# First norm of a transformer block on Trainium2: VectorE sums tiles 0, 1 and 3 and ScalarE tile 2, and two weight loads change places

## The chip, the cores and the metric

One core of a Trainium2 chip. The experiments ran on three chips (e1 to e4, e5 to e8, and e9 to e12), each group with the kernel before beside it. The metric is the device time of one execution in microseconds (us). A run in the "fast" state is one without a visible slowdown of the chip. Executions of one kernel differ by about 0.1% (the kernel before: 830.95 to 832.09 us), and the trace of single executions ("looks": one profiled execution of each kernel) has to show the mechanism.

## The reference

```python
x   = A_x                                   # 2048 rows of 1024, bf16
mod = silu(c) @ w_mod                       # six vectors: sa, ca, ga, sb, cb, gb
h   = layernorm(x) * (1 + ca) + sa          # "the first norm"
qkv = h @ wqkv
...                                         # linear attention, 32 heads, with elu+1 features
x   = x + ga * attention(...)
h   = layernorm(x) * (1 + cb) + sb
x   = x + gb * ((silu(h @ w_gate) * (h @ w_up)) @ w_down)
```

## The kernel before

The rows are worked in four chunks of four tiles of 128 rows. Only the head of the program is changed: the first norm of chunk 0, and the loads in front of the q products. For each tile a statistic, a term `(var + eps) ** -0.5` (a power on GpSimd), and a normalisation are made; TensorE transposes the tile; the scale `1 + ca` is multiplied in when the transposed tile is copied out of PSUM. The scale itself is made by TensorE in one-column products (`mod_sc`), from the weights `WCA` in two halves of 512 columns. `warm` issues dummy matmuls. A k-tile is 128 of the 1024 columns over which a product sums, so q's products need the scaled tile and the weights of all eight k-tiles.

```python
ca_load(0)                 # scale weights, columns 0-511
wq_load(0, 2)              # q weights, k-tiles 0, 1
ca_load(1)                 # scale weights, columns 512-1023
wq_load(2, 2)
wq_load(4, 2)
sa_load(1)                 # shift weights
...
warm(13, bank=3)
act_stats(1)               # ScalarE: sum and sum of squares of tile 1
for f in s0_: f()          # VectorE: statistics of tile 0
ln1_rstd1(0)               # its term
s2_[0](); s2_[1]()         # VectorE: statistics of tile 2
act_xn(0, MV[:, 0, 0:1])   # ScalarE normalises tile 0; VectorE makes its bias first
tile_transposes(0)
warm(5, bank=3)
act_var(1)
s2_[2]()
...                        # terms of tiles 1 and 2
s3_[0](); s3_[1](); s3_[2]()
ln1_rstd1(3)
act_xn(1, SUMX[:, 1:2])
ln1_xn(2)                  # VectorE normalises tile 2
tile_transposes(2)
mod_sc(WCA, 8, range(2))   # first scale columns (0-255)
ln1_xn(3)
fin_ca(0, 2)
tile_transposes(1, 3)
mod_sc(WCA, 8, range(2, 4))  # second scale columns (256-511)
h0_first(0, "dve")
...
# q products of chunk 0
for nts, dts in ((range(4), (0,)), (range(4), (1,)), ((4, 5, 6), (0, 1))):
    for nt in nts: q_part(nt, qb[nt], dts)
mod_sc(WCA, 8, range(4, 8))  # columns 512-1023
fin_ca(4, 4)
for dt in (4, 5): h0_scale_only(dt)
for nt in range(7): q_part(nt, qb[nt], (2, 3))
```

VectorE runs its instructions in the order written here.

## Time and profile before

| | before |
|---|---|
| time, median of 3 | 831.19 us (831.15 to 832.09) |
| span of the profiled execution | 829.4 us |
| TensorE busy | 824.0 us |
| first transpose of tile 0 | 8.76 us |
| first q product | 12.43 us |

The head of the profile page of the kernel before, busy time of each engine with its share of the span:

```profile
PE 824.0 (99%) x4083; PEld 378.4 (46%) x4083; DVE 312.0 (38%) x665; ACT 197.6 (24%) x336; POOL 39.8 (5%) x57
```

TensorE is busy practically always. So the question for any change here is not how much work VectorE loses, but when TensorE's unbroken work begins and what is in it.

TensorE's timeline of the kernel before: start, length, what it ran and how often, and in brackets the idle time before it with what ended that.

```profile
2.61 5.72 PE L176 MATMUL ps<-e,ident 128*128 128x512 bf16 x13 [0.24 <-DVE e L176]
8.76 0.62 PE L176 MATMUL ps<-ident,xres 128*128 128x128 bf16 x8 [0.42 <-ACT xres L176]
9.21 1.24 PE L176 MATMUL ps<-e,ident 128*128 128x512 bf16 x5
10.29 0.61 PE L176 MATMUL ps<-ident,xres 128*128 128x128 bf16 x8
10.74 0.54 PE L176 MATMUL ps<-siluc,wca 128*128 128x1 bf16 x16
11.14 1.05 PE L176 MATMUL ps<-ident,xres 128*128 128x128 bf16 x16
12.03 0.54 PE L176 MATMUL ps<-siluc,wca 128*128 128x1 bf16 x16
12.43 3.18 PE L176 MATMUL ps<-ht,wqk 128*128 128x512 bf16 x14
15.45 0.94 PE L176 MATMUL ps<-siluc,wca 128*128 128x1 bf16 x32
16.25 4.91 PE L176 MATMUL ps<-ht,wqk 128*128 128x512 bf16 x22
```

Lines `ps<-e,ident` are dummies, `ps<-ident,xres` transposes, `ps<-siluc,wca` scale columns, and `ps<-ht,wqk` q products. From 8.76 us on each line starts where the one before it has issued its last, with no idle time: five dummies fill 9.21 to 10.29 us, and 22 matmuls of 512 columns fill 16.25 to 21.00, 216 ns each.

The chain of waits of the kernel before, from its start in order of time (start, length, what). `xres` is a tile of rows, `stats` its statistics, `mv` their aggregate (mean and variance), `ve` the variance plus eps, and `nmr` the bias of ScalarE's normalisation:

```profile
1.71 4.21 DMA xres<-in_A_x_dram
...
5.94 1.29 DVE stats L176 x2
7.22 0.11 DVE nmr L176
7.34 0.14 DVE mv L176
7.47 1.23 ACT xres L176
...
8.76 818.08 PE ps L176 x4069
```

The chain reads: tile 2 lands at 5.92 us, VectorE takes its statistics, only then makes the bias of tile **0** (`nmr`), ScalarE normalises tile 0, and TensorE starts.

The DMA view of the kernel before, for the one issue at 2.65 us (KB, and us from issue to landing):

```profile
wca<-in_w_mod_dram SPq DMA_DIRECT2D x1, 1024.0 KB, 7.8
```

The first half of the scale weights landed at about 2.65 + 7.8 = 10.45 us, 0.3 us before its use at 10.74.

### The profile page before, as it was taken

How to read it: one execution, taken by the hardware profiler on the slowest of the kernel's cores; microseconds unless marked ns; L12 is line 12 of the kernel's file. 1: busy time of each engine (PE TensorE's matmuls, PEld its weight loads, DVE VectorE, ACT ScalarE, POOL GpSimd, SP SyncE). 2: the span in 40 equal slices, each digit the busy share in tenths (PEclk: the TensorE clock that was granted, in tenths of full speed). 3: DMA queues.
4: the chain of work that ended last, by engine and by line, in shares of the span. 5: the costliest groups of instructions: out<-in, count | busy, mean ns of one | idle time of the engine just before them, and what ended most of it. 6: DMA issues, size and time to landing. Idle time of an engine off the chain costs nothing.

```text
span 829.4 us, 10017 instructions
## 1 busy us (share of the span) xinstructions
PE 824.0 (99%) x4083; PEld 378.4 (46%) x4083; DVE 312.0 (38%) x665; ACT 197.6 (24%) x336; POOL 39.8 (5%) x57
## 2 busy tenths in 40 slices
PE   8999999999999999999999999999999999999998
PEld 4544444454444444444444444444444444444444
DVE  5797986756955521121221111122111111221111
ACT  4757641323242111011111101111110111111011
POOL 1010000000130000030000003000000300000000
PEclk9999999999999999999999999999999999999999
DMA  9969655928397996700455570045557004553000
GB/s 320 288 151 229 149 159 172 202 102 304 60 258 225 259 267 174 192 25 14 128 150 155 150 188 28 15 126 153 153 153 187 26 18 125 154 151 86 0 26 26
DMA packets 199245, 119.28 MB, mean 144 GB/s; under 512 B 57880, under 2 KB 182944, under 8 KB 199200
## 3 DMA queue, kind: packets, MB, share of 16 engines
q1 hardware_dynamic: 199184, 118.65, 52.7%
q8 instruction: 32, 0.52, 0.3%
q14 instruction: 13, 0.11, 0.0%
q10 hardware_dynamic: 16, 0.00, 0.0%
HBM read 100.67 MB, written 4.33 MB: 127 GB/s over the span
## 4 chain that ended last, share of the span: by engine, by line
PE 99%; DMA 1%; DVE 0%; ACT 0%; SPq 0%; issue 0%
PE ps L176 99%; DMA xres<-in_A_x_dram 1%; DVE stats L176 0%; ACT xres L176 0%; SPq L176 0%; DVE xres L176 0%; DVE mv L176 0%; DVE nmr L176 0%
## 5 line engine op out<-in xcount | busy, mean ns | idle before, releaser
L176 PE MATMUL ps<-h2t,gug 128*128 128x512 bf16 x896 | 211.7, 379 | 0.0
L176 PE MATMUL ps<-h2t,guu 128*128 128x512 bf16 x896 | 211.7, 379 | 0.0
L176 DVE TENSOR_TENSOR at<-sg,ps 128x512 bf16<-128x512 bf16 x112 | 77.1, 688 | 282.7 <-PE ps L176 281.1
L176 ACT ACTIVATE sg<-ps 128x512 bf16<-128x512 f32 x112 | 66.9, 597 | 309.7 <-PE ps L176 309.7
L176 PEld LDWEIGHTS ps<-h2t,guu 128*128 128x128 bf16 x896 | 87.5, 98 | 105.8
L176 PEld LDWEIGHTS ps<-h2t,gug 128*128 128x128 bf16 x896 | 87.4, 98 | 105.7
L176 PE MATMUL ps<-wd_a,at 128*128 128x512 bf16 (+1 forms) x512 | 112.4, 378 | 0.0
L176 PE MATMUL ps<-ht,wqk 128*128 128x512 bf16 x512 | 111.7, 379 | 0.0
L176 PE MATMUL ps<-wd_b,at 128*128 128x512 bf16 (+1 forms) x384 | 85.0, 378 | 0.0
L176 PEld LDWEIGHTS ps<-wd_a,at 128*128 128x128 bf16 x512 | 50.0, 98 | 59.8
L176 DVE TENSOR_TENSOR ut<-att,gb_b 128x512 bf16<-128x512 bf16 (+1 forms) x32 | 13.8, 430 | 167.5 <-ACT att L176 167.5
L176 PEld LDWEIGHTS ps<-ht,wqk 128*128 128x128 bf16 x512 | 49.4, 98 | 58.8
L176 ACT ACTIVATE att<-ps 128x512 bf16<-128x512 f32 (+1 forms) x32 | 17.4, 591 | 182.1 <-PE ps L176 182.1
L176 PEld LDWEIGHTS ps<-wd_b,at 128*128 128x128 bf16 x384 | 37.5, 98 | 44.7
L176 PE MATMUL ps<-pk,xres 128*128 128x512 bf16 x256 | 56.5, 379 | 0.0
L176 PE MATMUL ps<-mw,pqt 128*128 128x512 bf16 x256 | 56.3, 379 | 0.0
L176 POOL TENSOR_SCALAR h2t<-h2t,modcol 128x512 bf16<-128x512 bf16 x32 | 26.4, 841 | 383.0 <-DMA h2t<-xn 383.0
L176 ACT ACTIVATE e<-ps 128x512 bf16<-128x512 f32 x56 | 33.1, 603 | 31.7 <-PE ps L176 20.5
L176 PEld LDWEIGHTS ps<-mw,pqt 128*128 128x128 bf16 x256 | 24.8, 98 | 30.3 <-DVE xres L176 0.4
L176 PEld LDWEIGHTS ps<-pk,xres 128*128 128x128 bf16 x256 | 24.8, 98 | 30.0 <-issue 0.4
L176 ACT ACTIVATE junk<-xres 128x1024 bf16<-128x1024 bf16 x24 | 25.4, 1058 | 35.1 <-DVE xres L176 34.9
L176 DVE SCALAR_TENSOR_TENSOR xres<-ps,xres 128x512 bf16<-128x512 f32 x32 | 21.4, 689 | 12.3 <-PE ps L176 11.7
(107 smaller groups left out, 346.0 us busy)
## 6 DMA issues: line engine op xcount, KB each, us to landing
gug<-in_B_w_gate_dram SPq DMA_DIRECT2D x56, 512.0 KB, 3.9
guu<-in_B_w_up_dram SPq DMA_DIRECT2D x56, 512.0 KB, 5.2
xres<-in_A_x_dram SPq DMA_DIRECT2D x20, 256.0 KB, 7.8
rb<-recip_den SPq DMA_DIRECT2D x8, 512.0 KB, 11.5
stgx<-in_w_mod_dram SPq DMA_DIRECT2D x2, 2048.0 KB, 7.8
wd_a<-in_B_w_down_dram SPq DMA_DIRECT2D x4, 1024.0 KB, 7.8
out_dram<-xres SPq DMA_DIRECT2D x31, 128.0 KB, 1.7
xres<-in_A_x_dram SPq DMA_DIRECT2D x3, 1024.0 KB, 14.0
```

Source lines behind the costliest of these rows:

```text
L176: return getattr(e, method)(**kw)
```

## The change

The intent: VectorE takes tiles 0 and 1 as soon as they land, back to back, and makes both terms in one step; ScalarE takes tile 2; two dummies fewer; the q weights of k-tiles 2 and 3 are loaded ahead of the second scale half, and that half is used after the first six products of those k-tiles.

```diff
         ca_load(0)
         wq_load(0, 2)
+        wq_load(2, 2)
         ca_load(1)
-        wq_load(2, 2)
         wq_load(4, 2)
@@
         warm(13, bank=3)
-        act_stats(1)
-        for f in s0_:
+        act_stats(2)
+        for f in (s0_[0], s0_[1], s1_[0], s1_[1], s0_[2], s1_[2]):
             f()
-        ln1_rstd1(0)
-        s2_[0]()
-        s2_[1]()
-        act_xn(0, MV[:, 0, 0:1])
-        tile_transposes(0)
-        warm(5, bank=3)
-        act_var(1)
-        s2_[2]()
-        ...                      # terms of tiles 1 and 2
+        ln1_rstd2(0)
         s3_[0]()
         s3_[1]()
+        act_xn(1, MV[:, 1, 0:1])
         s3_[2]()
         ln1_rstd1(3)
-        act_xn(1, SUMX[:, 1:2])
-        ln1_xn(2)
-        tile_transposes(2)
+        ln1_xn(0)
+        tile_transposes(0)
+        warm(3, bank=3)
         mod_sc(WCA, 8, range(2))
+        act_var(2)
+        ...                      # term of tile 2
         ln1_xn(3)
+        tile_transposes(1)
+        ...                      # VectorE normalises tile 2
         fin_ca(0, 2)
-        tile_transposes(1, 3)
+        tile_transposes(3, 2)
         mod_sc(WCA, 8, range(2, 4))
@@
-            mod_sc(WCA, 8, range(4, 8))
-            fin_ca(4, 4)
-            for dt in (4, 5):
-                h0_scale_only(dt)
             for nt in range(7):
+                if nt == 3:
+                    mod_sc(WCA, 8, range(4, 8))
+                    fin_ca(4, 4)
+                    for dt in (4, 5):
+                        h0_scale_only(dt)
                 q_part(nt, qb[nt], (2, 3))
```

## The prediction

> **What bounds the kernel now.** TensorE. The page has it busy 824.0 of 829.4 us, and the chain of waits gives it one unbroken piece of 818.1 us from 8.76 us on. Its timeline shows no hole: in the q products 22 matmuls fill 16.25 to 21.00 us, 216 ns each, which agrees with the 215.7 ns of the Trainium skill (TensorE: Matmul & The Clock Gate, "Wait — 56ns, not 53.3ns?"). So a change in the first 30 us can only move the start of the dense stretch, take filler from it, or open holes.
>
> **The filler.** After tile 0's transposes (8.76) stand five dummy matmuls, to 10.29 us. Then come tile 2's transposes, the first scale columns (10.74 to 11.14), tiles 1 and 3 (to 12.03), more columns, and q at 12.43.
>
> **What the change does.** It removes two dummies (2 x 0.216 us). ScalarE's statistics (2.34 us for a tile) move from tile 1, landed 4.25, to tile 2, landed 5.92, and end near 8.28. With VectorE's durations from its timeline (statistics 0.65, aggregate 0.21, term 0.15, normalise 0.53; GpSimd's power 0.70 for two): tile 1's statistics end near 6.15, both terms' power near 7.4, tile 3's statistics near 7.9, tile 0 is normalised near 8.8. ScalarE normalises tile 1 at 8.3 to 9.55; tiles 3 and 2 are ready near 9.7 and 10.5.
>
> New TensorE order: tile 0's transposes 8.83 to 9.28, three dummies to 9.93, then the first scale columns. Their weights' issue plus time to landing is 2.65 + 7.8 = 10.45 us, and nothing moves ahead of them in the queue. So TensorE waits about 0.5 us: the removed dummies become a wait for a DMA. Columns to 10.87, tile 1 to 11.32, tiles 3 and 2 to 12.2, more columns, q near 12.6. Between the first columns and q stood 1.29 us of work; now 1.74, as one tile's transposes move behind them, while the columns start only 0.27 us earlier. Net: q starts **0.2 us later**.
>
> **The weights.** Landings came in issue order (10.4, 11.8, 14.8, 16.1: scale half, q 0-1, scale half, q 2-3), as the skill says of descriptors (DMA: Bandwidth & Descriptors, "HWDGE ordering"). q 2-3 landed 16.1 against its use at 16.25: just in time, costing nothing. Swapped, it should land near 13.2 and the scale half near 16.1, used near 16.9. No wait on either; the swap adds margin, not time. Later loads (shift halves landed 20.5 and 24.8, used 21.0 and 25.3) keep theirs.
>
> **On the critical path:** all of the 0.2 us, 0.02% of the time, below the spread of the three runs (0.9 us).
>
> **Prediction: 831.4 us, 8 in 10 within 830.5 to 832.5.** Faster by over 2%: 0.005; within 2%: 0.985; slower by over 2%: 0.01.
>
> **What would show it.** Right: TensorE's waits list about 0.5 us on the scale weights' DMA and about 0.5 us on VectorE before tile 0's transposes; q starts at 12.4 to 12.8 us and is dense after; no wait for q weights; the chain starts with the scale weights' DMA. Wrong in the step on the scale weights: no such wait, q near 12.1 us. Wrong in the swap: a hole near 17 us or at the shift columns.
>
> **What would make it wrong.** The scale weights landing earlier or later than 10.45; TensorE's clock not released in time after the longer pauses (dummies before 8.33 us ran at 426 ns each), costing up to a few us; a hole opened by a load whose place in the queue moved.

## The result, and the profile after

| | before | after |
|---|---|---|
| time, median of 6 | 831.21 us (830.95 to 832.09) | 831.24 us (830.69 to 831.44) |
| span of the profiled execution | 829.4 us | 829.6 us |
| first transpose of tile 0 | 8.76 us | 9.28 us |
| first scale columns | 10.74 us | 10.38 us |
| first q product | 12.43 us | 12.52 us |

The ratio is 0.9998, with a 95% interval of 0.9985 to 1.0011: the same. A ratio is the mean time of one kernel's fast runs over that of the other's of the same rounds, so it is not quite the ratio of the medians.

The head of the profile page after:

```profile
PE 823.7 (99%) x4081; PEld 378.8 (46%) x4081; DVE 312.1 (38%) x664; ACT 196.3 (24%) x335; POOL 40.2 (5%) x57
```

TensorE's timeline after:

```profile
2.61 5.73 PE L176 MATMUL ps<-e,ident 128*128 128x512 bf16 x13
9.28 0.62 PE L176 MATMUL ps<-ident,xres 128*128 128x128 bf16 x8 [0.94 <-DVE xres L176]
9.73 0.81 PE L176 MATMUL ps<-e,ident 128*128 128x512 bf16 x3
10.38 0.54 PE L176 MATMUL ps<-siluc,wca 128*128 128x1 bf16 x16
10.78 1.50 PE L176 MATMUL ps<-ident,xres 128*128 128x128 bf16 x24
12.12 0.54 PE L176 MATMUL ps<-siluc,wca 128*128 128x1 bf16 x16
12.52 4.48 PE L176 MATMUL ps<-ht,wqk 128*128 128x512 bf16 x20
16.84 0.94 PE L176 MATMUL ps<-siluc,wca 128*128 128x1 bf16 x32
17.64 3.61 PE L176 MATMUL ps<-ht,wqk 128*128 128x512 bf16 x16
```

Two dummies are gone, and q still starts 0.09 us later, because the transposes of tile 0 start 0.52 us later, after an idle time of 0.94 us. From there it is dense: 0.45 us of transposes, 0.65 of dummies, 0.40 of columns, 1.34 of transposes, 0.40 of columns, then q.

TensorE's waits after (who waited for whom: us in total, times, longest):

```profile
PE ps L176 <- DVE xres L176: 0.9, 1, 0.9
```

The chain of waits after, its first part:

```profile
2.18 4.84 DMA xres<-in_A_x_dram
...
7.04 1.29 DVE stats L176 x2
8.33 0.11 DVE nmr L176
8.44 0.14 DVE mv L176
...
8.61 0.15 DVE ve L176
8.76 0.47 DVE xres L176
...
9.28 817.77 PE ps L176 x4067
```

Now tile 3 (landed at 7.02 us) stands where tile 2 stood: VectorE takes tile 3's statistics, then tile 1's bias, tile 3's aggregate and term, and only then normalises tile 0. The wait for the scale weights that the prediction put at 10.45 us is absent. The DMA view after, for the issue at 2.65 us:

```profile
wca<-in_w_mod_dram SPq DMA_DIRECT2D x1, 1024.0 KB, 7.5
```

They landed at 2.65 + 7.5 = 10.1 us, and the columns behind the dummies were due at 10.38. The weights of k-tiles 2 and 3 landed at 12.9 us for a use at 15.54, the second scale half at 15.9 for a use at 16.84: as predicted, no wait.

The span grew by 0.2 us, q's start by 0.09. The rest is a small hole near 45 us, where chunk 1's products start. Busy time in the stretch from 43 to 47 us (length, then busy us and number of instructions of PE, PEld, DVE, ACT, POOL, then clock, DMA share, GB/s), first before, then after:

```profile
43.00:47.00 4.00, 4.00 (x20) 1.76 (x18) 4.00 (x15) 3.87 (x8) 0.00 (x0) 1.00 0.47 172
```

```profile
43.00:47.00 4.00, 4.00 (x19) 1.66 (x18) 4.00 (x15) 3.46 (x7) 0.00 (x0) 1.00 0.45 164
```

Both are "busy" for the whole 4.00 us, because matmul records overlap, but after it there are 19 matmuls against 20. The starts of single matmuls show it: two steps of 0.24 and 0.32 us instead of 0.22, 0.13 us in all, where the seventh and the eighth k-tile of the scaled chunk came late from VectorE (scaled until 45.11 and 45.43 us, used from 45.17 and 45.49). The sum closes with the end of the program, which was 0.03 us shorter behind VectorE's last step (2.55 against 2.58 us).

### The profile page after: what moved, and what is told of

It reads as the page before. It is cut to its first block, busy times and chain, and to the rows that moved or that the text cites. A ratio compares the mean times of both kernels' runs of the same rounds, so it can differ in the third digit from the quotient of the medians.

```text
span 829.6 us, 10010 instructions
## 1 busy us (share of the span) xinstructions
PE 823.7 (99%) x4081; PEld 378.8 (46%) x4081; DVE 312.1 (38%) x664; ACT 196.3 (24%) x335; POOL 40.2 (5%) x57
## 4 chain that ended last, share of the span: by engine, by line
PE 99%; DMA 1%; DVE 0%; SPq 0%; issue 0%
PE ps L176 99%; DMA xres<-in_A_x_dram 1%; DVE stats L176 0%; SPq L176 0%; DVE xres L176 0%; DVE ve L176 0%; DVE mv L176 0%; DVE nmr L176 0%
## 5 line engine op out<-in xcount | busy, mean ns | idle before, releaser
L176 DVE TENSOR_TENSOR at<-sg,ps 128x512 bf16<-128x512 bf16 x112 | 77.0, 688 | 282.8 <-PE ps L176 281.2
```

The lines of the kernel that those rows point to most:

```text
L176: return getattr(e, method)(**kw)
```

## The experiments

Three theories stand at the start. **A**, the prediction's: the landing of the first scale half is the floor under q's start. **B**, which the trace after suggests: VectorE's order ties tile 0 to tile 3's landing. **C**: the start doesn't matter much, because a later floor takes the difference. The looks are one execution each. This table collects what decides, with landings as issue time plus time to landing; "second columns" is the last work ahead of q, which follows 0.40 us later.

| kernel | tile 3 landed | tile 0's transposes | scale half landed | first columns | second columns | span | median time |
|---|---|---|---|---|---|---|---|
| before | 6.6 | 8.76 | 10.4 | 10.74 | 12.03 | 829.4 | 831.21 |
| after | 7.0 | 9.28 | 10.1 | 10.38 | 12.12 | 829.6 | 831.24 |
| e1_norm_only | 6.4 | 8.66 | 9.7 | 9.76 | 11.51 | 829.3 | 831.02 |
| e2_swap_only | 6.3 | 8.32 | 9.4 | 10.30 | 11.59 | 829.2 | 831.11 |
| e3_no_dummies | 6.9 | 9.19 | 9.8 | 9.86 | 11.65 | 829.4 | 832.10 |
| e4_eight_dummies | 6.3 | 8.64 | 9.4 | 10.83 | 12.57 | 829.9 | 831.98 |
| e5_tile0_first | 6.6 | 7.52 | 10.3 | 10.31 | 12.06 | 829.5 | 831.16 |
| e6_pair | 5.9 | 8.61 | 10.5 | 10.55 | 12.30 | 830.6 | 831.57 |
| e8_half_swap | 7.3 | 9.51 | 10.3 | 10.61 | 12.36 | 830.2 | 831.70 |

The kernel before was timed again beside each group: medians 831.75 (e1 to e4), 831.15 (e5 to e8) and 831.22 us (e9 to e12). Not one of the twelve is faster or slower than before by a clear amount; all 95% intervals contain 1 and lie within 0.3% of it.

### e1_norm_only: the norm without the swap

```diff
 wq_load(0, 2)
-wq_load(2, 2)
 ca_load(1)
+wq_load(2, 2)
# and the second scale half used before k-tiles 2, 3 again
```

> The changed kernel with the weight swap undone (loads and their use in the old order): the norm part alone. Theory A (the swap only adds margin): q's first matmul within 0.3 us of the changed kernel's 12.52 us; the k-tile 2, 3 products start near 16.3 us, right at their weights' landing near 16.1 us, with a hole of at most 0.1 us; time within 0.3 us of the changed kernel. Rival B (the swap is what kept the change from being slower): a hole of 0.3 us or more before the k-tile 2, 3 products, and a span 0.3 us or more above the changed kernel's 829.6 us. If the first scale weights' landing is what decides (the prediction's step), TensorE's waits name it; if tile 3's landing decides (what the trace after shows), they name VectorE before tile 0's transposes, 0.5 us or more.

Time 831.02 us, ratio 0.9991 (0.9976 to 1.0006). No hole before the k-tile 2, 3 products: their weights landed at 15.4 us for a use at 15.73. Theory A of this run, that the swap only adds margin, holds. Two of its figures missed: the second columns, and so q, stood 0.6 us earlier than in the changed kernel and not within 0.3, and the wait for VectorE was 0.33 us and not 0.5 or more. The code ahead of the second columns is the same; they came earlier because tile 3 landed 0.62 us earlier: the transposes of tile 0 moved by exactly that. The span gained only 0.3 us, as the hole near 45 us grew to 0.4 us.

### e2_swap_only: the swap without the norm

```diff
 wq_load(0, 2)
+wq_load(2, 2)
 ca_load(1)
-wq_load(2, 2)
# and the second scale half used after six products of k-tiles 2, 3
```

> The kernel before with the weight swap alone. Theory A: q starts at 12.4 us as before; q k-tiles 2, 3 land near 13 us, the second scale half near 16 us and is first used near 16.7 us; no hole in TensorE; time and span within 0.2 us of before. Rival B (landing 0.1 us ahead of its use was a hidden cost): 0.1 us or more faster in the span.

Time 831.11 us, ratio 0.9993 (0.9978 to 1.0008). The k-tiles 2, 3 landed at 12.1 us, the second scale half at 15.1 for a use at 16.3. The span is 0.2 us shorter, as the rival had it, but q started 0.44 us earlier for a reason outside the swap: tile 2 landed at 5.47 us instead of 5.92, and tile 0's transposes followed it 2.84 us later in both looks. So the swap itself shows no gain.

### e3_no_dummies and e4_eight_dummies: none, and eight, instead of three

```diff
-warm(3, bank=3)
+(nothing)            # e3
+warm(8, bank=3)      # e4
```

> The changed kernel without the three dummies after tile 0's transposes. Theory A (the first scale weights, landing at 10.1 to 10.45 us, are the floor right behind the dummies): the 0.65 us of dummies turn into a wait of 0.35 to 0.7 us on that DMA, and q starts 0 to 0.3 us earlier than 12.52. Rival B (TensorE's own work is the floor): q starts 0.6 us earlier, near 11.9 us, span 829.0.

> The changed kernel with eight dummies instead of three: 5 x 0.216 = 1.08 us more TensorE work ahead of everything. Theory A (TensorE is dense from tile 0's transposes on, so each dummy costs its full length): q starts 1.0 to 1.1 us later, near 13.6 us, and the span is 0.9 to 1.1 us longer, near 830.6 us. Rival (slack behind it, from loads or VectorE, takes it up): less than 0.5 us longer.

In e3's look the columns started at 9.86 us, 0.05 us after their weights had landed: 0.22 us of wait, and q 0.47 us earlier, between the two forecasts. But the span gained 0.2 us, and the times got worse: 831.13 and 831.60 us, and 833.24 and 832.61 us. The last two are the executions whose granted clock was 0.998 instead of 1.000. That is taken up again in e11.

In e4's look, against e1 (where tile 0's transposes started at the same time, 8.66 and 8.64 us), the second columns are 1.06 us later, the full length of five dummies. But the span is 0.3 us longer than after and 0.65 longer than e1's, not 0.9 to 1.1 longer than after. Both sums close. Against after, the second columns are only 0.45 us later, as tile 3 landed earlier, and the hole of 0.13 us is gone; against e1, the hole of 0.41 us is gone. The dummies do lie on TensorE's path, and a floor behind them takes part of what they cost.

### e5_tile0_first: tile 0 ahead of tile 3 on VectorE

```diff
-for f in (s0_[0], s0_[1], s1_[0], s1_[1], s0_[2], s1_[2]): f()
-ln1_rstd2(0)
+for f in s0_: f()
+ln1_rstd1(0)
+for f in s1_: f()
+ln1_rstd1(1)
+ln1_xn(0)
 s3_[0](); s3_[1]()
 act_xn(1, MV[:, 1, 0:1])
 s3_[2]()
 ln1_rstd1(3)
-ln1_xn(0)
 tile_transposes(0)
```

> The changed kernel, with tile 0's own term and its normalisation put ahead of tile 3's statistics on VectorE. Theory (VectorE's order ties tile 0's transposes to tile 3's landing: in the four looks at this order they began 2.25 to 2.30 us after it): the transposes begin right behind the 13 dummies, at most 0.15 us after their end, whatever tile 3's landing, instead of 2.26 us after it. Rival (tile 0 waits for ScalarE or GpSimd, not for that order): still 2.2 to 2.3 us after tile 3's landing. For the time: q's first matmul 0 to 0.6 us earlier than the changed kernel's (tile 2, ready near 10.8 us, or the scale weights hold it next), and of that no more than 0.3 us in the span, as products of chunk 1 near 45 us wait for their modulated tiles.

TensorE's timeline of this kernel:

```profile
7.52 0.61 PE L176 MATMUL ps<-ident,xres 128*128 128x128 bf16 x8
7.97 0.81 PE L176 MATMUL ps<-e,ident 128*128 128x512 bf16 x3
10.31 0.55 PE L176 MATMUL ps<-siluc,wca 128*128 128x1 bf16 x16 [1.52 <-DMA wca<-in_w_mod_dram]
```

The transposes start right behind the dummies, 0.93 us after tile 3's landing and not 2.26: theory B holds for tile 0. But q did not come earlier than after (12.46 against 12.52): the time went into a wait of 1.52 us for the first scale half, which landed at 10.26. That is the prediction's theory A, uncovered as soon as tile 0 was out of the way. In this look nearly all of the freed time was lost to the next floor. Time 831.16 us, ratio 1.0001 (0.9987 to 1.0015).

The table now gives one rule for all looks of the changed order. Tile 0's transposes start 2.25 to 2.30 us after tile 3's landing (or after 6.3 to 6.4 us, when VectorE has made the two terms, if that is later), the first columns start 1.10 us behind them with three dummies or 0.05 us after the scale half's landing, whichever is later, and q 2.14 to 2.16 us after that. In after and e8 the former decides, in e6 (a wait of 0.7 us for the scale half) and e5 the latter; in e1 the two meet. e9, e10 and e11, run later, keep to the first part (2.27, 2.25 and 2.26 us).

In this look the hole near 45 us was 0.42 us, two matmuls fewer than before in the same 4 us:

```profile
43.00:47.00 4.00, 4.00 (x18) 1.50 (x17) 4.00 (x13) 3.17 (x7) 0.00 (x0) 1.00 0.66 238
```

### e6_pair: two groups of chunk 1 interleaved

```diff
-for dt in range(8): matmul(bank[0], k-tile dt)
-for dt in range(8): matmul(bank[1], k-tile dt)
+for dt in range(8):
+    for nt in range(2): matmul(bank[nt], k-tile dt)
```

> The changed kernel, with the first two product groups of chunk 1 interleaved by k-tile, so that TensorE uses the eight k-tiles in 3.4 us instead of 1.7, slower than VectorE makes them (0.33 us each). Theory (the hole near 45 us, 0.13 us in the changed kernel's trace and 0.4 us where q started earliest, is the second floor): no hole at 44 to 47 us (under 0.03 us), so the span is q's start plus 816.9 us or less; the span falls by the size of the hole, 0.1 to 0.4 us, with q's start unchanged. Rival (the hole only moves to another buffer): another hole of the same size between 44 and 65 us.

No hole near 45 us. But this says little: in this execution q started 0.18 us later and TensorE waited 0.7 us up to 22.1 us for the shift weights, which landed at 22.05 instead of 20.2, so chunk 1's products came late anyway. Inconclusive. Time 831.57 us, ratio 1.0002 (0.9987 to 1.0018). It shows something else: the shift weights are a further load with under a microsecond of margin (0.9 us after, landing to use), and can fall behind it without any change to their place.

### e8_half_swap: loads in the new order, use in the old

```diff
 # on the changed kernel
-for nt in range(7):
-    if nt == 3: mod_sc(WCA, 8, range(4, 8)); ...
-    q_part(nt, qb[nt], (2, 3))
+mod_sc(WCA, 8, range(4, 8)); ...
+for nt in range(7): q_part(nt, qb[nt], (2, 3))
```

> The changed kernel with the loads in the new order but the second scale half used where it was before, ahead of the k-tile 2, 3 products. Theory (loads and their use have to move together; the swap costs and gains nothing by itself): the scale columns, due 3.0 us after q's start (15.0 to 15.5 us), wait for a landing at 15.1 to 16.1 us: a hole of 0 to 0.7 us there, equal to landing minus due time, named as a wait on the scale weights' DMA. Rival (no hole): the second scale half lands before 15.0 us and the move of its use was not needed.

TensorE's timeline of this kernel:

```profile
12.76 3.18 PE L176 MATMUL ps<-ht,wqk 128*128 128x512 bf16 x14
16.12 0.95 PE L176 MATMUL ps<-siluc,wca 128*128 128x1 bf16 x32 [0.18 <-DMA wca<-in_w_mod_dram]
```

The half landed at 16.07 us, its columns were due at 15.78 and started at 16.12: 0.34 us of hole, 0.29 from due time to landing and 0.05 from there to the start, named as a wait for that DMA. (The view's 0.18 counts from the modelled end of the last matmul, 12.76 + 3.18.) The theory holds: load order and order of use have to be moved together. Time 831.70 us, ratio 1.0005 (0.9991 to 1.0019).

### e9_less_work and e10_less_work_pair: 0.8 us of work taken away before chunk 1

```diff
-bias_mm((4, 5)); bias_mm(range(4))
+bias_mm((4,));   bias_mm((3,))       # a wrong bias on purpose
```

> The changed kernel with 32 of its 48 one-column bias products left out (a wrong result on purpose): 32 x 0.025 = 0.8 us less TensorE work at 23 to 28 us, between the first norm and chunk 1. Theory (the modulated tiles of chunk 1 are a second floor near 45 us, with at most 0.3 us of slack behind it in the traces of before and after): most of the 0.8 us comes back as a hole at 44 to 46 us, of 0.5 to 1.1 us, and the span falls by 0.3 us or less. Rival (TensorE's work before chunk 1 counts in full): no hole above 0.15 us and a span 0.7 to 0.8 us shorter.

> The same with the first two groups of chunk 1 interleaved by k-tile. Theory (second floor, which the interleaving moves 1.5 us later): the hole is 0.1 us or less and the span is 0.4 us or more shorter than without the interleaving, 0.7 to 0.9 us shorter than the changed kernel's. Rival: the same hole and span as without the interleaving.

Neither theory's numbers came: the span of e9 fell by little, as the theory had it, but not for its reason. (Both kernels still passed the comparison with the reference; the bias left out is small.) In e9 there was no hole near 45 us: the scaling of chunk 1 started at 40.9 us instead of 42.8, as VectorE's work ahead of it moved forward too. So the hole near 45 us is not a fixed point in time, as theory C had it; it seems to depend on when the chain of VectorE and DMA transposes runs. The products of all four chunks were done, and the next stage began, 1.17 us earlier than after (125.76 against 126.93 us). Not all of that is the work removed. q itself started 0.73 us earlier (tile 3 landed at 6.27 us), the hole of 0.13 us was gone, and of the 0.8 us removed 0.44 came back at once: the products due at 26.83 us waited until 27.27 for VectorE's copy of the bias (`biasq`), which stands behind a statistic in VectorE's order. And the span was only 0.2 us shorter. TensorE's and VectorE's timelines of e9 show this wait and where the rest went:

```profile
27.27 23.05 PE L176 MATMUL ps<-ht,wqk 128*128 128x512 bf16 x104 [0.28 <-DVE biasq L176]
...
229.12 2.12 PE L176 MATMUL ps<-mw,pqt 128*128 128x512 bf16 x9 [0.87 <-DVE xres L176]
```

```profile
225.77 2.29 DVE L176 TENSOR_REDUCE red<-mhlt 128x8 f32<-128x2048 bf16 x1 [0.88 <-DMA mhlt<-mhl]
```

At 225.8 us VectorE waited 0.88 us for a DMA transpose (`mhlt`), TensorE's PSUM banks were not emptied, and TensorE waited 0.87 us at 229 us. That transpose took 6.0 us from issue to landing in e9 and 5.9 in e10; in the twelve other looks it took 4.3. In e9 and e10 alone a transfer of 16 KB, of the kind that the trace calls `instruction`, began while it was under way (at 223.7 and 224.9 us; in the twelve others it began at 214.9 to 217.9, ahead of the transpose). So the wait may be a side effect of taking instructions away, but that is not tested, and a like transfer inside a later transpose of the same two looks (281.2 and 282.7 us) lengthened nothing. e10 had no hole near 45 us either, the same wait at 230 us, and late shift weights (a wait of 0.3 us up to 21.4), and was slower than e9 in all four executions: 831.71 to 832.35 us against 831.24 to 831.59. Whether the interleaving costs something is open. The times of both kernels say only this: 0.8 us of TensorE work removed, 0.44 of it given back at once, brought no gain clear of the noise (831.29 us, ratio 1.0000, 0.9986 to 1.0014, and 832.11 us, ratio 1.0008, 0.9992 to 1.0023).

### e11_long_pause: nine dummies at the start instead of thirteen

```diff
-warm(13, bank=3)
+warm(9, bank=3)
```

> The changed kernel with 9 dummies instead of 13 at the start, so that TensorE pauses for 2 to 3.5 us before tile 0's transposes. Theory (the dummies keep the clock up; without the later three, two of four executions were granted 0.998 of the clock and took 1.5 us longer): the granted clock falls below 1.000 in at least half of the executions, and those take 1 us or more longer. Rival (that was chance): 1.000 in all, and the changed kernel's time.

Time 832.29 us median, ratio 1.0013 (0.9998 to 1.0028), in single executions 830.73, 831.94, 832.63 and 834.35 us. The granted clock was 0.998 in two of the four (831.94 and 832.63), 0.7 and 1.4 us above after's median, so one of them misses the forecast of 1 us; the longest had 1.000, which this theory does not explain. The profiled execution was one with 0.998. TensorE's timeline of it:

```profile
8.93 0.62 PE L176 MATMUL ps<-ident,xres 128*128 128x128 bf16 x8 [2.47 <-DVE xres L176]
9.38 1.31 PE L176 MATMUL ps<-e,ident 128*128 128x512 bf16 x3
10.49 0.61 PE L176 MATMUL ps<-siluc,wca 128*128 128x1 bf16 x16
10.96 2.44 PE L176 MATMUL ps<-ident,xres 128*128 128x128 bf16 x24
13.24 0.54 PE L176 MATMUL ps<-siluc,wca 128*128 128x1 bf16 x16
```

After the idle time of 2.47 us the first transposes still ran at the full rate, 56 ns each. Then the clock fell: the second and the third dummy each took 427 ns to the next start instead of 216, and the 24 transposes behind the first columns took 2.28 us from first start to the next line, 107 ns each until 13.0 us, against 1.34 after. The trace's record of the granted clock says the same: half from 9.55 to 12.96 us, 3.41 us in the middle of the first norm. The Trainium skill (TensorE: Matmul & The Clock Gate, "What's actually happening") gives a free-running window of about 3.4 us and half the clock after at least one idle window. The length of the slow stretch agrees; the pause ahead of it, 2.47 us, was shorter than such a window. The estimate from the mean clock agrees too: 0.998 over 830 us is about 1.7 us lost, half of 3.4. So the dummies are no mere filler: with fewer of them the clock fell in two of four executions of e11 and in two of four of e3, and in no execution of another kernel for which the record lists a clock. That e3's two fell in the same way is likely and not shown, as its profiled execution was not one of them.

### e7_best and e12_best_again: what the experiments point to

```diff
 # e5, and in addition:
-act_xn(1, MV[:, 1, 0:1])     # ScalarE
+ln1_xn(1)                    # VectorE, behind tile 3's term
 tile_transposes(0)
 warm(3, bank=3)
+tile_transposes(1)           # ahead of the first scale columns
 mod_sc(WCA, 8, range(2))
 # and the interleaved pair of e6
```

> Tile 0's term and normalisation ahead of tile 3's statistics, tile 1 normalised by VectorE and transposed ahead of the first scale columns, and the pair of groups of the run before. Theory (two floors, the first norm's order and the modulated tiles of chunk 1, both taken away): q starts near 11.7 to 12.0 us, no hole near 45 us, span 828.7 to 829.0, 0.5 us below before (829.4 to 830.4 in its runs): 0.05 to 0.1%. Rival (a third floor: the shift weights' halves, landing near 20.5 and 25 us, cap the start of everything behind them): holes at 20.5 or 25 us that give back what q's start gains beyond 11.95 us.

> The kernel with both floors moved (tile 0's term and normalisation first, tile 1 on VectorE and transposed early, the interleaved pair), a second time. Theory: its executions again lie within 0.5 us of each other near 830.8 us, 0.3 to 0.5 us below before. Rival (the first time was a lucky chip state): median within 0.1 us of before.

Both gave the lowest median times, in narrow ranges: 830.78 us (830.76 to 831.12; ratio 0.9996, 0.9983 to 1.0008) and 830.76 us (830.71 to 830.96; ratio 0.9993, 0.9981 to 1.0006), with spans of 829.0. By the intervals that is the same as before. And the theory gets no credit for it. q started at 12.39 and about 12.33 us, only 0.04 and 0.1 us earlier than before, not at 11.7 to 12.0. In e7 TensorE was idle for 0.8 us before tile 1's transposes and 0.4 before tile 2's: VectorE had become the floor, and for tile 2 the two powers on GpSimd ahead of its normalisation (9.11 to 10.52 us in the chain). The last step of the program (VectorE's last addition) started at 826.81 and 826.74 us, against 826.86 before. The remaining 0.35 us comes behind it: from there to the end of the span it is 2.21 and 2.22 us, against 2.58 before and 2.55 after. e5 has the same short end (2.23); in the nine remaining looks it was 2.55 to 2.59. The head of e7's page shows what sets these three programs apart, the count of GpSimd's instructions (POOL), 58 and not 57:

```profile
PE 823.0 (99%) x4081; PEld 378.8 (46%) x4081; DVE 313.2 (38%) x665; ACT 195.0 (24%) x334; POOL 40.7 (5%) x58
```

e5, e7 and e12 make the terms of tiles 0 and 1 by two powers instead of one; the eleven others have 57. The traces also show where the time lies: GpSimd's last two semaphore instructions are 0.08 to 0.09 us apart in the three and 0.41 to 0.43 in the eleven. And a transfer of 8 KB of the kind `instruction` (queue q14), which begins behind the end of the span in the eleven (829.8 to 831.4 us), begins at 650.6 to 651.3 in the three. So the shorter end goes with one more instruction on GpSimd and not with either floor. No run adds that instruction alone, so this stays unproven as a cause.

## Why the prediction was right or wrong, point by point

- **The verdict and the time were right.** 831.4 was forecast, 831.24 measured, in the range; the same, as forecast. For the profiled execution this was in part luck: tile 0's transposes came 0.45 us later than forecast (9.28 against 8.83), and the wait of about 0.5 us behind them did not come. The two misses cancel.
- **"TensorE is dense; a change can only move the start, take filler, or open holes" was right.** The trace after shows the start of the dense part moved from 8.76 to 9.28 us, two dummies fewer, and a hole of 0.13 us.
- **"Net: q starts 0.2 us later" was right in direction and about right in size** (0.09 us), **but for another reason in the execution that was profiled.** The step that failed is "So TensorE waits about 0.5 us: the removed dummies become a wait for a DMA". There, the removed dummies became a wait for VectorE, 0.94 us before tile 0's transposes (forecast as about 0.5), as tile 3 landed at 7.02 us and not at 6.6. The scale half landed at 10.1 and not at 10.45, so the columns, due at 10.38, didn't wait. The forecast had used the landings of the one trace before as if they were fixed: put into e5's rule, those landings (6.58 and 10.44 us) give q at 12.63 us, the forecast's 12.6. Over all fourteen looks tile 3 landed between 5.9 and 7.3 us and the scale half between 9.3 and 10.5; e5 and e6 show the forecast wait, 1.5 and 0.7 us, the profiled execution after doesn't.
- **"The chain starts with the scale weights' DMA" was wrong** for after (it starts with tile 3's landing) and right for e5.
- **"The swap adds margin, not time" was right.** e1 and e2 show no hole that the swap makes or removes; e8 shows that half of the swap opens a hole of 0.34 us.
- **"All of the 0.2 us on the critical path" was too simple.** Of the 0.2 us by which the span grew, 0.09 is q's start and 0.13 is the hole near 45 us (the end took back 0.03). In e1 that hole took back 0.4 us of a start 0.6 us earlier.
- **The risk of the clock was rightly named.** It didn't strike the changed kernel: all six executions had a clock of 1.000. e11 strikes it on purpose.

Where the expected gain of the change went: two dummies (0.43 us) and a quicker pair of tiles were paid in, and tile 0's transposes gave it back by waiting for tile 3's landing, behind statistics that VectorE's order puts first. When that was undone (e5), the first scale half's landing held the columns. When tile 1 was moved ahead of the columns as well (e7), VectorE's work on tile 1 and GpSimd's powers ahead of tile 2 held TensorE.

## What to carry to other kernels

When the head of a kernel is held by several loads that land within a microsecond of each other, read the due time and the landing of every one of them: removing the last wait uncovers the next, and a forecast from one trace's landings can name the wrong one and still get the time right. A tiny instruction inherits the wait of everything in front of it on its engine, so look at what stands before the first result that another engine needs. And before you remove dummy matmuls, check the granted clock of every execution: they may be holding it.

## What the Trainium skill lacked or had wrong

- TensorE: Matmul & The Clock Gate, "Why this matters for your kernels", advises no TensorE pauses above about 3 us. In e11 a pause of 2.47 us, followed by a little light work, was enough for 3.41 us at half rate (transposes at 107 ns instead of 56); a pause of 2.25 us in e3's profiled execution was not.
- The same page's "Part 4: PE-mode transpose" says that the full clock does not engage for transposes. Here they ran at the full rate, 56 ns each, whenever the dummies ahead had released it (in after from 9.28 us on); in e11 the clock even came back at 13.0 us, in the midst of transposes.
- DMA: Bandwidth & Descriptors has no figure for how much landings of the same load vary between executions. The first scale half, 1 MB in the same place of the queue, landed between 9.3 and 10.5 us; the first shift half between 20.1 and 22.1. Its "HWDGE ordering" says that a later DMA may complete before an earlier one; in every look the order of landing was the order of issue for all SyncE's loads of the first 28 us.
- The same page gives no time from issue to landing for a DMA transpose from SBUF to SBUF. The one of `mhlt` near 221 us took 4.3 us in twelve looks and 5.9 and 6.0 in the two with less bias work; the one near 280 us took 5.4 to 7.6 us.
- No page has a figure for what a program's end costs with one instruction more or less on an engine (it would belong to Runtime: NRT & Kernel Launch). From the last VectorE step to the end of the span it took 2.21 to 2.23 us in the three programs with 58 GpSimd instructions and 2.55 to 2.59 us in the eleven with 57.
